# An attention-then-experts kernel: the last query group normalised in two parts, and a new hand-written order of instructions

## The chip, the core and the metric

The kernel runs on one core of a Trainium2 chip. The metric is the device time of one execution in microseconds (us), as the median of several executions. Work is spread over five engines with a queue each: TensorE (PE; its weight loads are shown as PEld), VectorE (DVE), ScalarE (ACT), GpSimd (POOL) and SyncE (SP), which here only issues DMAs. ACT can issue DMAs too.

## The reference

What is computed: attention of 8 batches of 12 heads with 448 positions of 64 values, whose q and k are first normalised, and behind it a mixture of 8 experts. Each expert takes the 448 tokens with the highest gate values for it, one expert after the other, and the tokens go through two matrix products.

```python
def _attn_ref(q, k, v, g_q, g_k):
    q_n, k_n = rmsnorm(q, g_q), rmsnorm(k, g_k)
    scores = q_n @ k_n.T / sqrt(64)
    scores = scores - max(scores, axis=-1)
    attn = exp(scores)
    attn = attn / (sum(attn, axis=-1) + 1e-9)
    return attn @ v
...
def _moe_ref(x, w_gate, w1, w2):
    logits = x @ w_gate                       # 3584 tokens, 8 experts
    for idx in argsort(-logits.flatten()):    # tokens to experts, 448 each
        ...
    for e in range(8):
        out[mask] = relu(x[mask] @ w1[e]) @ w2[e]
```

## The kernel before

Attention comes first (0 to 416 us), then the choice of the tokens (the router) and the experts; each expert's lists are found beside the products of the expert before it. Only attention is touched by the change.

Attention works on 24 groups of four heads (`g` 0 to 23; a group is two pairs of heads, a batch is three groups). For each group q and k are loaded, squared (`square`, L301) and summed on DVE (`sumsq`, L307), and a reciprocal root is made (`rsqrt`: two ACT steps at L313 and L315, then three small DVE or POOL steps, L319 to L326). Then come the scaling (`norm`, L342; q also times the gains, `gain`, L368 to L371) and the split into two 16-bit halves (`hi` on ACT, L376; `lo`, L379). From the third group on the halves are turned by DMA transposes (`transpose`, L389); the first two groups are worked in halves (`a` 0 and 1) and turned on PE (`turn_first`, L402), for an early start. PE then multiplies q and k once for the row maxima (`max_score`, L504 and L507, reduced on DVE at L514) and once exactly (`scores`, L535 to L544); ACT takes the exponentials (`exp`, L550).

`av` (L569) multiplies the exponentials with v. For one pair of blocks (`pair` 0 to 47, two for each group) it fills one PSUM tile `po` in seven windows `w`, sixteen matmuls each. When all seven are there, the pair is normalised: `x_norm` in three steps on DVE (the sums at L582, the reciprocal at L584, the product in place at L586), then `x_hi` on ACT (L596) writes the upper 16-bit half into `xa`, and `x_lo` on DVE (L602) the rest. `x_store` sends `xa` to memory in four DMAs for each batch, for the experts' gathers.

For the last batch (b = 7, pairs 42 to 47) there is a tail. `x_turn(7, hp)` turns, on PE, three of the windows of two pairs (L634; for odd `hp` also the window in the middle, L637): `hp` 4 takes windows 0 to 2 of pairs 46 and 47, `hp` 5 windows 4 to 6 and window 3 of the same pairs. `x_turned` copies the result (ACT, L652, for `hp` below 4, else DVE, L654). `gate_last` (L684 to L686) makes the gate's products with it in six steps, and `gate_copy` (L698, L699) hands the logits to the router, whose first instruction is L1124.

What runs when is not left to a scheduler. `plan` lists all 2117 steps of attention with their conditions; `ORDER` is a string of two characters for each step, and `Plan.run` emits the steps in just that order. Each engine works its steps in the order emitted and waits where a step needs another engine's result. So moving a step moves it in its engine's queue and decides for what everything behind it waits.

The first loads of q are issued by SP, the first loads of k by ACT: two main loads (192 KB, L235) and two tails (32 KB, L227) each. The first half of group 0 needs the first main load and both tails; the second half needs the other main load. Both queues also load a small gain vector (`gain_loads`, L141).

Of the kernel before, what the change touches and what calls it, by code (L numbers as in the profile page):

```python
# [31 lines left out]
OP = mybir.AluOpType  # L32
# [57 lines left out]
class Attention:  # L90
# [497 lines left out]
    def x_parts(self, pair):  # L588
        b, hp = divmod(pair, 6)
        x = self.T["xa", b].rearrange("p (w i h d) -> p w i h d", i=2, h=6, d=64)  # L590
        return self.T["po", pair][:, :, :64], x[:, :, 0, hp], x[:, :, 1, hp]

    def x_hi(self, pair):
        x, h, _ = self.x_parts(pair)
# [5 lines left out]
    def x_lo(self, pair):  # L600
        x, h, l = self.x_parts(pair)
        self.nc.vector.tensor_tensor(l, x, h, op=OP.subtract)  # L602
# [118 lines left out]
    def plan(self):  # L721
# [114 lines left out]
        for pair in range(2 * self.NG):  # L836
            b, hp = divmod(pair, 6)
            add("xn0", "D", 0.17, self.x_norm, pair, 0, after=[("po", pair)], make=("z", pair),
                opens=[("z", pair)] + [("xb", b)] * (hp == 0))
            add("xn1", "D", 0.2, self.x_norm, pair, 1, after=[("z", pair)], make=("y", pair), uses=[("z", pair)])  # L840
            add("xn2", "D", US["xn"], self.x_norm, pair, 2, after=[("y", pair)], make=("xn", pair), uses=[("z", pair)])
            add("xhi", self.engine("xhi", pair), US["xhi"], self.x_hi, pair, after=[("xn", pair)], make=("xh", pair), uses=[("xb", b)],
                frees=[("po", pair)])
            add("xlo", "D", US["xlo"], self.x_lo, pair, after=[("xh", pair)], make=("x", b, hp), uses=[("xb", b)],
                frees=[("po", pair)])
            x = [("x", b, n) for n in range(6)]
            if hp == 5:
                for i in range(4):
                    add("xst", "S", 0.6, self.x_store, b, i, after=x, uses=[("xb", b)], move=(1.5, 0.32 if i > 1 else 1.9))
                if b < last:  # L850
                    for i in range(4):
                        add("xtr", "S", 1.9 if i < 3 else 1.2, self.x_dma_turn, b, i, after=x, opens=[("xt", b)] if i == 0 else (),
# [10 lines left out]
            if b == last:  # L863
                ring = ("pm", "psc")[hp % 3 > 0]
                add("xturn", "T", US["xturn"], self.x_turn, b, hp, after=[x[hp | 1], x[hp - hp % 2]],
# [14 lines left out]
    def plan_first(self, plan, g, a):  # L880
# [47 lines left out]
        "050204031506160z1718191A0+1B0708000-1C1E1G1c1F1H1d1I1J1e1K1f1L091g1h1i1N1D1b1M011P1R242122252326281k1j1O1Q2x2z"  # L928
        "2-2y302+123M3N1n2A1o1l1m2W1U1S292B1TBZ2X2C2D1V2Y1W2E312ZBa2a2bBbBf1pBc2c1sBd1qBe32272V2F2G2H331u2I2e2d2J1rBh2h"
        "2f2i2K2g2L3OBg1X1Y1t342MBi2N353637BnBl14131z1Z1aBo2jBm2kGtGuBj2OBkBp39383ABqGvBr3Q2l3RBs1v1wGwBv3B3C3D3E0A1+3m"  # L930
        "3n0B0C1x1yBw2P2m2o2QGxBtGzGyX4G+Bu3P3S3o3q3TBxByG-H0BzB+M7MDMAM83p3F10C3C4MCC1C2B-H1H2C02R2pH3C52nC6M9MBRN3UH4"
        "3V3Y3W3X3a3bC7ROC83rME2S2q2T2r4A2sMGC9MF2UH5CACBCCRPMKH7CDCEMJMHMICF4BCG3s4C3tH6H83G2u2v202w1-2tRQRRH9HBHA3c4Y"
        "4ZCHCIHDRSHCHE3Z3d3u3w3v4a3y3H0D3I3JCJCKMLMNMRCL4DCM3x3+4E4F3KHFHGHHHICNCORTRUMMMOMQCPCQRV4cRW3z0E3-403L4G4HMP"
        "HJCRCSHL4KHKHMMSCTMTMYMWMX4dCUCVHN4bHOCWRXRYHPHQ3e3fMUCXRZCYHRMVCZ4eRaHS4fRb4I4L4J4M3gHVHTCaCbRc0FCcRd4NReMZMb"
        "MdCdHUHWRfCeRgMaHX4y4+CfCgMfMgMjCh4zCiMmMeMi4g4h414k4-Mc4O5K3lCjCkRhRiHZ5L4i4j4l3h3jHY3kHa4m3i0G4nHb4243444P4o"
        "MkClRjRkCmMhHd50HcCnRlCoMl4546He51525453RmRnHfCpCqRoHh4748HgHiMnCrRpCsHj4p49HlCtMsMtMrCuRqRvRuRyCvCwHkHm5M5O5N"
        "HnHpCxCyHo5PMoMpMqMu4Q4RS3Hr56HqHsCzS4C+11MyMvM+C-D0S5HtHxD1D2554S6658595A57MzMxMw4TD35QHu5RS65kS7S8S9D4SAHvHw"
        "Hy5mM-N5D5N4N3D6HzD75lD8N2H-4qSB4VSC4rH+I05n5o5p5S5T4U5W5U5V4WI15YI2D9DAN6N1N7NCDBDCN0SDI3I4685q5ZDDSEDESFNANB"
        "N8DFDGI5SGI6SHI7DHDIN9SISJRxRr67Rw5X5r5sI9DJDKSKI8IA5B4sIBICSLRzR+R-DLDMSMID6AIF5uIEIGRs5a4X6u6vDNDO69S0S15t5v"
        "4tNDNENH5C5DS2IHDPDQ6BNFNKNMDRNINGDS5w6W5xII6C4v4w6D6E6F4u6GIJDVNJILIKIMDWDTDUSNSOSPSQNNNPNQDXINIO5E5bIPIQDYDZ"  # L940
        "DaSRNLIR5yDbDc6X6H6I6K6LNONRNUNTSSSTRt4x5J5F6JIS5cIT5dSUSVDdDeSWNXIVDfNWNYNeDgNdDhNbNSNV5H6Y6ZIU6w6a6b5IIW5z6c"
        "6d5eDiDjSlSmDkSn5GIXIYIZDlDmSoSp6e6f0HNZNaNcDnIbIaSbSaId6gIc6yIe5f6hDo6xSqSr5+5-SsStNfNjNi6MDpDqIfIg5hIhDr6z7I"
        "6+6-70Ii6i6j72735g0I0JDsSuNlNgNhNkDtSvDuIjIkSc5jSdSeSfSgShSwSxSyDvDwIl7KImInSzDxSi5iSjDyNmNsNoDzNnNpNrNq7LD+D-"
        "S+S-E0Sk7g6k606NSXIp6l616462710KIoIrE1E2T0IqIsNtNuNw6O6P7JT1T2ItE3E4NyNxNvNzT3747M767N7O77757P7QN+O0E7T4E8T5Iv"
        "IuIwT6IxIy63E5E6O3N-O1E9T7EAIz65I+I-EBECO2O4T87RJ07iJ1T9TA6R6S6TJ2TBEDEEO5O7O66mTC6n7j7S6QJ3J47h6U7k78J5EFEGOC"
        "OEO8EHJ7O97UJ67V7TEIJ87l7mOAOBJ9EJSZ6VSYTHTI6oTK7WTRTSTTEK7nTUTVJBJAJCODOHENEOJDJF8486JEELEM85JGOJOGOOOIEPEQ87"
        "JHJIJJEROPOLESOFTWTXTYJL7A7BJK7o7q7p797sJNETEU7r7u7t0L7vTZJMJO8889TaTJ8S8T6p8A6s8B8C6qOMOKONTbTcEVEWTdJPJQ6rTL"
        "TNTMEXEYTeTfJRJTJSEbEcTOOQOVOUEZ8U8VEaJUTPTQ6t7CJXJVEd8D8W8s7XJW8E8GTGTE7w8IJY8FEeOXObOWEfOROTOdOS7D7EEg8X8Y8u"
        "8Z7GEhTgEiThJZJb7Y7ZTiOcEjEk8a8H8c8bJaTjJcTkOZOYOaTlElTmEmTn8vJdOeOgEnOjOkOhOfOiEo7FToJe7x8e8d8g8h8fTF7H7bTpEp"
        "TqTrEqJfJgJh7f7a9ETDErEsTsOlOrOnEtOqOoOmEu7yJiTtTu7zJj8t7+7c7e9GJkJlEvJm8w0M0NOsOpEwU79HOuOvExJnJoJpEyU8U97d8x"  # L950
        "UAJqEzOyE+UBOtOwOx0O8yE-UCF0UDUEJrJt9F9IJsJuUFF1F2OzP0O+P1F3UGF4JvJx8z8i8JTzU0T-T+83F5F68+8-0P9e9fJwJy0Q0R7-80"
        "9092P2O-P4P98K8L8MTx9JJz819KJ+J-F7F8P8P3P5P7UHUIUJK0UK9LF9FAULK1K3FBFC919M9NA0TyP6PA8N938O9OK2K49g8PU1U3U2UMUN"
        "UOFDFEK5K7UP82UQFFU4K6U5K8FGPBPEPGPHPDU69h9i9j9P8jFHFIPIPCPOFJA2A1A49QFKA3K98Q948RKAKB9SKCFLPFFMPNPJPLFNURUSUT"
        "UUFOKDKF8kUV8lTv958m9U9R8r9T0S0T0U0VPMPKUWUX0W0X8n8pKEKG8o9k0Y0Z0aFRFS0b9lKHKJKIKKFPUYFQPPPQPVFTFUKLKNUZUaUfUh"
        "KMFVFWPUPWPYFXKPKOKQFYKRKSFZFaPZKT8qKU96KV97TwUi9mKW9oAQ9nFbFcPcPXPSFdFeKXKYKZKa9qFhFiPRPTUpUqUrPaFfFg98KdKbUs"
        "UtFjFkPb9D9r999p9CKcKeA5UuUvA6A79BA80cAAABA90dPdPhPiPgFlKfKgFmUwUxKhKi9sFnFoUyPePjPfUz9W9XU+KjU-V0FpUgUjUlUkKl"
        "FqV1FrARFsUmPkPpPqPoPmUnUoFtFu0e9APrPnPwFvPxASATFwPlV29VACAEAF0fAD0gAoAq9YApAGV3V4AUAVAWKkKm9Z9aAXPsPtFxFyKn9d"
        "Uc9tV5V6KoKpFzF+PvPuV7Kr9uV8V99v9wUbUdAH9bKq9cKsKtF-ArG0PyQ2Q0P+G1AsVAVBKuG2KvKxG3G4AaKwAY0h0i0jAZAc0k0lKyAeUe"
        "Q1P-PzQ30mVCAtG5G6KzK+Q7Q9VDVEG7G89x0n0oAd0pAu9zVFAv9+VGVKVHK-L0AwAbAf9-VLVM9yL1L2BCBEAxAyAzG9GAQ5Q6QAQGGBGCBF"
        "L3L5L4GDGEQBQ8Q4QEQFVVVWVXL6VYAIL7L9L8AJAKAPVOGFBD0qVZQDGG0r0sQHQCALVaBGA+BHLAB0AOQIQJGHVbVcGILBLDVdVeLCLEGLGM"  # L960
        "QLQMQKGJGKAMA-BIBJB1BK0tQOQNQRQPGNLFLHVfVgVhViGOGPGQVjQTQQQUQSVkVlBMLGLIB2GRGSLJLLAgAhVmLKLMVNVPVRVQGTVJAiBLGU"
# [1036 lines left out]
```

## Time and profile before

| | us |
|---|---|
| three runs, median (lowest, highest) | 918.54 (917.5, 920.09) |
| the profiled execution, its own time | 916.3 |
| the profiled execution, span from first to last instruction | 914.5 |
| PE busy in the span | 863.1 |
| DVE, ACT, POOL busy | 660.6, 466.9, 343.0 |

The trace is of the profiled execution alone. A line of a timeline names start, duration, engine, line of the kernel, operation, what it writes and reads, and in brackets the idle time of that engine before it and what ended it. ACTq and SPq are the DMA-issuing parts of the ACT and SP queues. "Granted clock" (PEclk) is the TensorE clock as a share of full speed.

### The profile page before, as it was taken

What the parts mean: (1) busy time and instruction counts of PE and PEld (TensorE: products, weight loads), DVE (VectorE), ACT (ScalarE), POOL (GpSimd) and SP (SyncE); (2) the same over time, 40 slices, a digit from 0 to 9 for tenths busy, and PEclk for the clock granted to TensorE, in tenths of its full rate; (3) what the DMA queues carried; (4) which work ended last, traced back from release to release, by engine and by line L of the source; (5) the groups of instructions that cost most, each with busy time, mean ns of one, the idle gap of its engine ahead of it and who ended that gap; (6) DMA issues with size and microseconds to landing.
All of it is one profiled execution on the core that took longest, in us unless ns stands there. A gap on an engine that the chain in (4) does not pass through costs nothing.

```text
span 914.5 us, 30177 instructions
## 1 busy us (share of the span) xinstructions
PE 863.1 (94%) x13219; PEld 579.4 (63%) x13220; DVE 660.6 (72%) x1465; ACT 466.9 (51%) x670; POOL 343.0 (38%) x433
## 2 busy tenths in 40 slices
PE   2799999999999999995899999999999999999996
PEld 1367767777776777784556555565565655655873
DVE  5999878878886886647887777786858758149630
ACT  4777787788677676551333424232433324234411
POOL 6788787777675776100103021110112020121101
PEclk9999999999999999996899999999999999999999
DMA  6467999999998998621828559492929469461301
GB/s 198 113 157 173 183 261 156 219 179 224 205 230 182 210 203 143 114 82 63 253 86 251 182 190 268 150 282 91 298 88 282 142 219 258 155 130 69 131 18 44
DMA packets 224952, 157.31 MB, mean 172 GB/s; under 512 B 162100, under 2 KB 211508, under 8 KB 224820
## 3 DMA queue, kind: packets, MB, share of 16 engines
q1 hardware_dynamic: 219378, 132.90, 61.1%
q0 software_dynamic: 4608, 22.02, 7.0%
q8 instruction: 103, 1.69, 0.7%
q10 hardware_dynamic: 834, 0.46, 0.2%
q14 instruction: 29, 0.24, 0.1%
HBM read 94.40 MB, written 22.02 MB: 127 GB/s over the span
## 4 chain that ended last, share of the span: by engine, by line
PE 71%; issue 17%; DVE 5%; POOL 3%; DMA 2%; ACT 1%; SPq 1%; POOLq 0%; DVEq 0%
PE po L569 18%; PE ph L1775 16%; PE py L1792 13%; PE psc L535 9%; PE pm L504 4%; PE psc L537 3%; PE py L1801 2%; DVE mx L514 2%; POOL out_dram L1808 1%; POOL rows L1712 1%; DMA kqh<-s 1%; PE psc L542 1%; PE rp L1318 1%; DVE st L307 1%; PE rp L1475 1%
## 5 line engine op out<-in xcount | busy, mean ns | idle before, releaser
L514 DVE TENSOR_REDUCE mx<-pm 128x2 f32<-128x896 f32 x162 | 176.7, 1091 | 49.2 <-PE pm L504 44.8
L569 PEld LDWEIGHTS po<-v,e 128*64 128x64 f32 x5376 | 166.8, 137 | 31.8 <-issue 28.9
L569 PE MATMUL po<-v,e 128*64 128x65 f32 x5376 | 182.6, 223 | 2.9 <-issue 2.8
L1775 PE MATMUL ph<-xt,w1h 128*128 128x448 f16 (+2 forms) x708 | 183.5, 343 | 0.4 <-DVE xt L1733 0.3
L550 ACT ACTIVATE e<-psc 128x896 f32<-128x896 f32 x168 | 148.6, 912 | 49.9 <-PE psc L537 39.3
L1808 POOL DMA_INDIRECT out_dram<-y,idx x32 | 34.4, 1075 | 307.9 <-ACT y L1794 279.3
L1792 PE MATMUL py<-w2h,hh 128*128 128x384 f16 x384 | 125.0, 326 | 0.0
L1792 PE MATMUL py<-w2h,hl 128*128 128x384 f16 x384 | 125.0, 326 | 0.0
L1792 PE MATMUL py<-w2l,hh 128*128 128x384 f16 x384 | 125.0, 326 | 0.0
L1775 PE MATMUL ph<-xt,w1l 128*128 128x448 f16 (+2 forms) x354 | 119.9, 343 | 0.0
L1792 PEld LDWEIGHTS <-hh 128*128 128x128 f16 x768 | 73.6, 97 | 45.6
L1775 PEld LDWEIGHTS <-w1h 128*128 128x128 f16 x708 | 64.7, 97 | 52.7 <-issue 1.5
L1764 ACT ACTIVATE hh<-ph 128x448 f16<-128x448 f32 x56 | 30.5, 544 | 125.8 <-PE ph L1775 122.7
L1794 ACT ACTIVATE y<-py 128x384 f32<-128x384 f32 x48 | 23.5, 490 | 116.2 <-PE py L1792 96.0
L1712 POOL DMA_INDIRECT rows<-xd,idx x32 | 31.0, 969 | 114.9 <-DVE idlo L1480 46.8
L1579 DVE SCALAR_TENSOR_TENSOR w2l<-stage,w2h 128x768 f16<-128x768 f32 x64 | 60.2, 951 | 8.6 <-ACT w2h L1575 8.6
L504 PE MATMUL pm<-kqh 64*64 64x448 f16 x588 | 56.7, 362 | 1.8 <-DMA kqh<-s 1.4
L535 PE MATMUL psc<-kqh 64*64 64x448 f16 x588 | 56.0, 353 | 0.8 <-issue 0.4
L537 PE MATMUL psc<-rowq,rowk 64*64 64x448 f16 x588 | 55.8, 349 | 0.7 <-issue 0.7
L1766 DVE SCALAR_TENSOR_TENSOR hl<-ph,hh 128x448 f16<-128x448 f32 x56 | 34.1, 617 | 30.9 <-ACT hh L1764 30.8
L307 DVE TENSOR_REDUCE st<-sq 128x14 f32<-128x910 f32 (+2 forms) x52 | 52.7, 1016 | 4.4 <-ACT sq L301 4.4
L535 PE MATMUL psc<-kql,kqh 64*64 64x448 f16 x588 | 55.4, 349 | 0.0
(301 smaller groups left out, 1620.8 us busy)
## 6 DMA issues: line engine op xcount, KB each, us to landing
stage<-in_moe_w_dram SPq DMA_DIRECT2D x64, 768.0 KB
vraw<-in_v_dram SPq DMA_DIRECT2D x21, 448.0 KB
xd<-xa SPq DMA_DIRECT2D x16, 576.0 KB
qkraw<-in_q_dram SPq DMA_DIRECT2D x10, 896.0 KB
qkraw<-in_k_dram SPq DMA_DIRECT2D x10, 896.0 KB
xd<-xa SPq DMA_DIRECT2D x16, 96.0 KB
vraw<-in_v_dram SPq DMA_DIRECT2D x3, 384.0 KB
qkraw<-in_k_dram SPq DMA_DIRECT2D x2, 384.0 KB
```

The lines of the kernel that those rows point to most:

```text
L307: self.nc.vector.tensor_reduce(self.stat(g, 0, a)[:, i], self.view(self.T["sq", g, i], a), axis=AX.X, op=OP.add)
L504: self.nc.tensor.matmul(o, mine, self.every(k, r, a), start=True, stop=True)
L514: self.nc.vector.tensor_reduce(m, p[r, :, :448], axis=AX.X, op=OP.max)
L535: mm(o, mine, self.every(q, r, n), start=i == 0, stop=False)
L537: mm(o, one[r, :64], self.every(row, r, n), start=False, stop=True)
L550: self.nc.scalar.activation(e, p[:, :, :448], AF.Exp, scale=scale)
L569: self.nc.tensor.matmul(po[o:o + 64, w], self.T["e", d][:, h, q:q + 64], self.v32[g % 2][:, h, 4 * a + d % 7 % 4], start=d == ds[0], stop= ...
L1579: self.later(0.93, lambda w=w: self.nc.vector.scalar_tensor_tensor(l[:, w], v[:, w], self.WS, h[:, w], op0=OP.mult, op1=OP.subtract), k, i)
L1712: nc.gpsimd.indirect_dma_start(out=g[:n, c, :], out_offset=None, in_=self.xd, in_offset=bass.IndirectOffsetOnAxis(ap=idx[:n, c:c + 1], axi ...
L1775: nc.tensor.matmul(p, a, b[:, o], start=st, stop=sp)
L1792: nc.tensor.matmul(p, a[:, f, s], b[:, f, o], start=st, stop=sp)
L1808: st = nc.gpsimd.indirect_dma_start(out=self.out, out_offset=bass.IndirectOffsetOnAxis(ap=self.router.out[k][:n, c:c + 1], axis=0), in_=y[ ...
```

## The change

Three things are changed. First, pairs 46 and 47, the last group, are normalised in two parts: windows 0 to 3 (part 0) and windows 4 to 6 (part 1); each of the five steps of a pair is issued once for each part. Part 0 waits only for the first four windows of `av`, and the steps behind it (`x_turn` with `hp` 4 and three of the four stores of the batch) only for part 0. All earlier pairs are done as before. Second, ACT issues the load of the gain vector ahead of its four loads of k, not between them. Third, the string `ORDER` is new as a whole, with 2127 steps, ten more than before.

```diff
+    def windows(self, part):
+        return slice(0, 7) if part is None else slice(4 * part, 4 + 3 * part)
-    def x_norm(self, pair, n):
+    def x_norm(self, pair, n, part=None):
...
-        po = self.T["po", pair]
-        if n == 0:
+        w = self.windows(part)
+        po = self.T["po", pair][:, w]
+        if n == 0 and not part:
...
-        z = self.T["z", pair]
+        z = self.T["z", pair][:, :, w]
...
-            V.tensor_tensor(po[:, :, :64], po[:, :, :64], z[:, 1, :, None].to_broadcast([128, 7, 64]), op=OP.mult)
+            V.tensor_tensor(po[:, :, :64], po[:, :, :64], z[:, 1, :, None].to_broadcast([128, w.stop - w.start, 64]), op=OP.mult)
...
-                    after=[("VF", g), *(("e", d) for d in ds)], make=("po", pair),
+                    after=[("VF", g), *(("e", d) for d in ds)], make=("po", pair, int(w > 3)),
...
+            for part in (0, 1) if pair >= 2 * self.NG - 2 else (None,):
+                y, f = (pair, part), 1.0 if part is None else 0.6
+                po = [("po", pair, i) for i in ((0, 1) if part is None else (part,))]
+                add("xn0", "D", 0.17, self.x_norm, pair, 0, part, after=po, make=("z", *y),
...
-                    add("xst", "S", 0.6, self.x_store, b, i, after=x, uses=[("xb", b)], move=(1.5, 0.32 if i > 1 else 1.9))
+                    add("xst", "S", 0.6, self.x_store, b, i, after=done(int(i == 1)), uses=[("xb", b)], move=(1.5, 0.32 if i > 1 else 1.9))
...
     ORDER = (
-        "050204031506160z1718191A0+1B0708000-1C1E1G1c1F1H1d1I1J1e1K1f1L091g1h1i1N1D1b1M011P1R242122252326281k1j1O1Q2x2z"
...
+        "150501030207060z1716180+04000-191A1B1C1E1c1F08091d1D1b1G1H1I1J1eXE1K1f1L1g1h21242322281225262x2+301+2y1N1M1P1i"
...
```

Read out, the string says this of the places that matter.

Start, ACT's queue, before: load of k (main), load of k (tail), gain vector, tail, main, then squares of q half 0, k half 0, q half 1. After: gain vector, main, tail, tail, main, then squares of q half 0, q half 1, k half 0. The step `unit` (L439) moves from between the third and the fourth exponential up to the squares. On DVE the sum of q half 1 and the router's constant `before` (L1005), which stood behind the sum of k half 0 and behind `norm`, move ahead of the sum of k half 0. SP issues gq's load second instead of third, and the first load of v ahead of the last tails of group 1. On POOL the `gain` steps of group 1 move ahead of the last `lo` step of group 0.

Tail, PE's queue, after the last scores, before: `av` of pair 46 (six windows), pair 47 (four), then mixed to the end; then `x_turn` 1, 2, 3, and 5 and 4 among the gate steps. After: pair 46 windows 0, 1, 3, 2; `x_turn` 1; pair 47 windows 0, 2, 1, 3; pair 46 windows 4, 5, 6; pair 47 windows 4, 6, 5; `x_turn` 3, 4, 2; gate steps 0 and 1; `x_turn` 5; gate steps 4, 3, 2, 5. On DVE, behind the last `av`, the steps are: sums and reciprocal of pair 47 part 1, `x_lo` of pair 46 part 1, the product of pair 47 part 1, the copy of `x_turn` 4, `x_lo` of pair 47 part 1, and the two copies of `x_turn` 5.

Between `av`, scores and gate steps PE changes over 286 times in the old order and 286 times in the new one.

## Rows read from the trace of the kernel before

**Rows 1.** Busy time in stretches: PE, PEld, DVE, ACT, POOL us (instructions), clock, DMA.

```profile
20.00:40.00 20.00, 14.16 (x131) 7.82 (x128) 18.86 (x26) 13.85 (x28) 15.80 (x18) 1.00 0.34 112
40.00:60.00 20.00, 18.07 (x372) 12.07 (x364) 18.44 (x23) 15.68 (x30) 15.71 (x19) 1.00 0.59 126
```

**Rows 2.** Busy time of PE from 60 to 404 us, us (matmuls), clock, DMA.

```profile
60.00:404.00 344.00, 337.64 (x8522) 1.00 0.92 189
```

**Rows 3.** Timeline of ACT and SP at the start, DMA issues and first squares.

```profile
2.04 0.68 ACTq L141 DMA_DIRECT2D gk<-in_g_k_dram  x1
...
2.76 0.61 SPq L227 DMA_DIRECT2D qkraw<-in_q_dram  x1
...
4.75 0.60 ACTq L227 DMA_DIRECT2D qkraw<-in_k_dram  x1
5.39 0.61 ACTq L235 DMA_DIRECT2D qkraw<-in_k_dram  x1
6.12 0.63 ACT L301 ACTIVATE sq<-qkraw 128x512 f32<-128x512 f32 x1 [4.10 <-issue]
10.04 1.05 ACT L301 ACTIVATE sq<-qkraw 128x512 f32<-128x512 f32 x2 [3.29 <-DMA qkraw<-in_k_dram]
```

**Rows 4.** The chain that ended last, start to 44 us: start, duration, what.

```profile
10.78 0.71 DVE st L307
...
14.34 0.14 DVE before L1005
...
43.11 0.13 ACT unit L439
43.25 0.25 ACT unit L439
```

**Rows 5.** Timeline of DVE and POOL at 11 to 25 us: small root steps.

```profile
14.59 0.17 DVE L325 TENSOR_TENSOR st<-st 128x12 f32<-128x12 f32 x1
19.36 2.23 POOL L368 TENSOR_TENSOR qn<-qkraw,gg 128x512 f32<-128x512 f32 x2
19.64 1.02 DVE L324 TENSOR_TENSOR st<-st 128x16 f32<-128x16 f32 x1
20.70 0.92 DVE L325 TENSOR_TENSOR st<-st 128x16 f32<-128x16 f32 x1
24.21 0.95 DVE L324 TENSOR_TENSOR st<-st 128x12 f32<-128x12 f32 x1
```

**Rows 6.** Timeline around 270 us: a DMA transpose and PE's wait for it.

```profile
268.01 4.25 SPq L389 DMA_TRANSPOSE kqh<-s  x1
...
276.36 0.38 PE L504 MATMUL pm<-kqh 64*64 64x448 f16 x4 [1.45 <-DMA kqh<-s]
```

**Rows 7.** Timeline of the tail, from the last products to the router's first step.

```profile
404.02 6.75 PE L569 MATMUL po<-v,e 128*64 128x65 f32 x224
409.43 0.17 DVE L582 TENSOR_SCALAR z<-po 128x7 f32<-128x7 f32 x1 [5.24 <-PE po L569]
410.83 0.17 DVE L582 TENSOR_SCALAR z<-po 128x7 f32<-128x7 f32 x1 [0.33 <-PE po L569]
411.02 0.20 DVE L584 RECIPROCAL z<-z 128x7 f32<-128x7 f32 x1
411.26 0.63 DVE L586 TENSOR_TENSOR po<-po,z 128x448 f32<-128x448 f32 x1
411.93 0.54 ACT L596 ACTIVATE xa<-po 128x448 f16<-128x448 f32 x1 [0.18 <-DVE po L586]
412.50 0.62 DVE L602 TENSOR_TENSOR xa<-po,xa 128x448 f16<-128x448 f32 x1
413.22 0.49 PE L634 MATMUL psc<-ident,xa 128*128 128x128 f16 x6 [0.37 <-ACT xt L652]
414.80 0.56 DVE L654 COPY xt<-psc 128x768 f16<-128x768 f16 x1 [0.17 <-PE psc L634]
416.53 0.18 DVE L698 COPY logits<-po 128x24 f32<-128x24 f32 x1 [1.18 <-PE po L686]
```

More of the change, by code (lines that the diff above doesn't have):

```diff
@@ L585, in x_norm, with x_parts, x_hi @@
         else:
-            V.tensor_tensor(po[:, :, :64], po[:, :, :64], z[:, 1, :, None].to_broadcast([128, 7, 64]), op=OP.mult)
-    def x_parts(self, pair):
+            V.tensor_tensor(po[:, :, :64], po[:, :, :64], z[:, 1, :, None].to_broadcast([128, w.stop - w.start, 64]), op=OP.mult)
+    def x_parts(self, pair, part=None):
         b, hp = divmod(pair, 6)
[L590 to L594, printed above, removed]
+        w = self.windows(part)
+        x = self.T["xa", b].rearrange("p (w i h d) -> p w i h d", i=2, h=6, d=64)[:, w]
+        return self.T["po", pair][:, w, :64], x[:, :, 0, hp], x[:, :, 1, hp]
+    def x_hi(self, pair, part=None):
+        x, h, _ = self.x_parts(pair, part)
         if self.engine("xhi", pair) == "A":
@@ L598, in x_hi, with x_lo @@
             self.nc.vector.tensor_copy(h, x)
-    def x_lo(self, pair):
-        x, h, l = self.x_parts(pair)
+    def x_lo(self, pair, part=None):
+        x, h, l = self.x_parts(pair, part)
         self.nc.vector.tensor_tensor(l, x, h, op=OP.subtract)
@@ L837, in plan @@
             b, hp = divmod(pair, 6)
[L838 to L843, printed above, removed]
@@ L844, in plan @@
-            add("xlo", "D", US["xlo"], self.x_lo, pair, after=[("xh", pair)], make=("x", b, hp), uses=[("xb", b)],
-                frees=[("po", pair)])
-            x = [("x", b, n) for n in range(6)]
+            for part in (0, 1) if pair >= 2 * self.NG - 2 else (None,):
+                y, f = (pair, part), 1.0 if part is None else 0.6
+                po = [("po", pair, i) for i in ((0, 1) if part is None else (part,))]
+                add("xn0", "D", 0.17, self.x_norm, pair, 0, part, after=po, make=("z", *y),
+                    opens=([("z", pair)] + [("xb", b)] * (hp == 0)) * (not part), uses=[("z", pair)] if part else ())
+                add("xn1", "D", 0.2, self.x_norm, pair, 1, part, after=[("z", *y)], make=("y", *y), uses=[("z", pair)])
+                add("xn2", "D", US["xn"] * f, self.x_norm, pair, 2, part, after=[("y", *y)], make=("xn", *y), uses=[("z", pair)])
+                add("xhi", self.engine("xhi", pair), US["xhi"] * f, self.x_hi, pair, part, after=[("xn", *y)], make=("xh", *y),
+                    uses=[("xb", b)], frees=[("po", pair)])
+                add("xlo", "D", US["xlo"] * f, self.x_lo, pair, part, after=[("xh", *y)], make=("x", b, hp, part), uses=[("xb", b)],
+                    frees=[("po", pair)])
@@ L847, in plan @@
+            split = lambda n: 6 * b + n >= 2 * self.NG - 2
+            x = [[("x", b, n, i if split(n) else None) for i in range(2)] for n in range(6)]
+            done = lambda *parts: [x[n][i] for n in range(6) for i in (parts if split(n) else (0,))]
             if hp == 5:
                 for i in range(4):
-                    add("xst", "S", 0.6, self.x_store, b, i, after=x, uses=[("xb", b)], move=(1.5, 0.32 if i > 1 else 1.9))
+                    add("xst", "S", 0.6, self.x_store, b, i, after=done(int(i == 1)), uses=[("xb", b)], move=(1.5, 0.32 if i > 1 else 1.9))
@@ L850, in plan @@
                 if b < last:
                     for i in range(4):
-                        add("xtr", "S", 1.9 if i < 3 else 1.2, self.x_dma_turn, b, i, after=x, opens=[("xt", b)] if i == 0 else (),
+                        add("xtr", "S", 1.9 if i < 3 else 1.2, self.x_dma_turn, b, i, after=done(0, 1), opens=[("xt", b)] if i == 0 else (),
                             make=("xt", b, i), uses=[("xb", b), ("xt", b)], move=(1.5, 2.4 if i < 3 else 1.25))
@@ L864, in plan @@
                 ring = ("pm", "psc")[hp % 3 > 0]
-                add("xturn", "T", US["xturn"], self.x_turn, b, hp, after=[x[hp | 1], x[hp - hp % 2]],
+                add("xturn", "T", US["xturn"], self.x_turn, b, hp, after=[x[n][i] for n in (hp | 1, hp - hp % 2) for i in range(1 + hp % 2 if split(n) else 1)],
                     make=("tp", hp), opens=[("xt", b)] * (hp == 0), holds=[(ring, ("xt", hp))], uses=[("xb", b), ("xt", b)])
@@ L932 @@
[L932 to L961, printed above, removed]
@@ L967 @@
+        "GlGmLlLnLmLoBAGpGqWBWCWDQtQwQvQsGrLpLrGsWEWFBSBTQuQxQrBVLqR1Q+R0QyQzQ-WJWKWLWMBXLsLtLuBUW0VzLvLwWSWTWNWUWVW5W7"
+        "W6LxLzLyBYWWW8L+W9BWXDWAR2R3R7R6R8R4R5L-M1M0WGM2M3M4WaWbWcWdM5M6WeR9RARCRBWORGRIWjWkWlWPRHWmWnRJWwWxWyWHWzW+X4"
+        "X6X7RDRERFWoWpWqRKRMRLW-X0WrWQWsWfWhX1X2WgWtWuX3WXWIWRWYX9XBWvWiWZXAXCX8X5"
     )
```

43 lines of the change are left out of this document (35 added, 8 removed).

## The prediction

> **What bounds the kernel now.** I read the busy time in stretches first, to see which engine leads where. Up to 60 us DVE does: it is busy 18.86 of 20 us from 20 to 40 and 18.44 from 40 to 60, while PE has 14.16 and 18.07 [rows 1]. From there to the end of attention PE is the bound: 337.64 of 344 us, so 6.36 us of idle time in all [rows 2]. The steps on PE are the same before and after, and the number of its changes between kinds of work too (286). So the change can act in three places: the start, where DVE and what feeds it decide; the 6.36 us of stalls in the long middle; and the tail, where PE waits for the last pairs to be normalised. The router and experts behind are emitted as before and start when the logits are there.
>
> **The start.** The first half of group 0 needs k's main load and both tails. ACT's third load of k is issued only at 4.75, though the gain vector was done at 2.72, and the square of k waits until 10.04 for it; from there the chain runs on through DVE, from 10.78 [rows 3, 4]. What holds that issue the trace does not name. After the change it is still ACT's fourth DMA, with the gain vector (0.68) moved to the front. Bounds: it follows the others at once, at about 2.75, 2.0 us sooner, and if the way from issue to square stays 5.29 us (10.04 - 4.75) the chain gains 2.0. Or the whole queue slips by the vector's 0.68 and it loses 0.7. I take 0: the two loads ahead aren't what the square waits for, and the nearest row is the issue at 4.75 itself, the fourth in this queue as it will be again.
>
> The sum of q's second half goes ahead of k's. DVE is free there, as ACT waits 3.29 us for k before its next square [rows 3], and behind 10.78 that sum lay beside ACT's logarithm, so it gives nothing on the chain. The constant `before` goes the same way; its 0.14 us was on the chain [rows 4]. `unit` was on the chain too, 0.13 + 0.25 us between two exponentials [rows 4]; moved up to the squares it lies in ACT's waits for DVE. Together 0.5 us.
>
> The new order of POOL and DVE behind this can give or take more. Three small root steps on DVE took 1.02, 0.92 and 0.95 us, while POOL was at work, where a like one took 0.17 [rows 5]: 2.4 us on the leading engine. Each ended as a POOL step ended (19.64 + 1.02 = 20.66; POOL's two `gain` steps fill 19.36 to 21.59). In the new order POOL's `gain` steps of group 1 come one `lo` step earlier, but that `lo` step follows them at once, so POOL still has work without a gap as these root steps arrive. I take 0, between a gain of 2.4 (all three free) and a loss of 0.8 (one more caught). SP's loads change places too; the five that group 0 needs of it stay the first five, so I take 0.
>
> What DVE gains before 55 us moves PE's whole stream, as PE has the same work from there on. So the start is worth 0.5 us, from -1.0 to +3.
>
> **The middle.** Every queue gets a new order, SP's most of all: transposes, loads and stores change places. PE's stalls are single waits such as 1.45 us at 276.36 for a transpose that SP had issued at 268.01 and that took 4.25 us [rows 6]. Nothing in the string says that they become fewer or more as a rule: in nine groups before and six after, no PE step stands between the issue of the upper transpose and the first maximum that needs it. I take 0. The bounds are the 6.36 us at most gained, and as much lost; half of either is already a lot.
>
> **The tail.** Each pair in two parts means five small steps more for each of two pairs, 10 in all. Most cost nothing, as DVE was idle for 5.24 us beside the last products [rows 7]. What counts is the chain from PE's last product to the logits. Before: product done by 410.8, sum 0.17, reciprocal 0.20, product 0.63, ACT's half 0.54, `x_lo` 0.62, `x_turn` 5 at 413.22, that is 2.4 us; then 3.3 us more to 416.53, with the two turns, three copies and the gate steps in turn [rows 7].
>
> After: PE does `x_turn` 1 between the products now, about 0.6 us (0.49 for six transposes [rows 7], two more for the middle). It lay behind them in the shade of the chain before. 224 products take 6.75 us, 0.48 for a window, as before, so the last one ends at 411.4. Behind it on DVE: sum 0.17, reciprocal 0.20, then `x_lo` of pair 46, part 1, which stands ahead, the product of pair 47, the copy of `x_turn` 4 (0.56), and `x_lo` of pair 47. A step of three windows costs between 3/7 of the row for seven and the whole; I take some 0.6 of it: 0.37, 0.38, 0.37. With six gaps of 0.03 the sum is 2.25, so `x_turn` 5 starts at 413.65, later than now. But behind it less is left: the turn 0.6, two copies 0.25 and 0.56, one gate step instead of two (0.7), gaps 0.2: 2.3 us, so the logits come at 415.95 instead of 416.53. The tail gains 0.6; with 3/7 it gains 0.9, with the full durations it loses 0.2.
>
> There is one more cost that the trace of before can't show: both parts of a pair lie in one tile `po`, and the new order puts products of part 1 behind the vector steps of part 0. If the products wait for these (they write other columns), PE stands: four windows 1.93, `x_turn` 1 0.6, four windows 1.93 from 404.02 is 408.5; the part-0 steps of pair 47 (five, 1.6 to 2.4 us by the same scaling of [rows 7], with 4/7) end at 410.1 to 410.9; PE is done with part 1 of pair 46 at 409.95 and would wait 0.15 to 0.95 for pair 47. I take 0.1 as the forecast's share, as most of these steps lie beside the products of pair 46 and nothing yet shows the wait, and keep 0.95 for the range. The Trainium skill speaks here: its page "PSUM — Partial Sum Buffer", section "PSUM bank collisions raise a hardware error", says that two engines on one bank and the same partitions at once raise an error even at different columns, so that accesses have to be guarded by bank. By that rule the wait is there, and no run so far shows it.
>
> **The sum.** 0.5 at the start, 0 in the middle, 0.6 - 0.1 in the tail: 1.0 us. The profiled execution took 916.3 us (914.5 of span and 1.8 around it), so it would take 915.3. It lies 2.24 below the median of the three runs, 918.54, and below all three; I forecast for the median: 917.5.
>
> **The rivals.**
> First, k comes early: the fourth DMA of ACT isn't held any more. For it: the wait from 2.72 to 4.75 stands right behind the gain vector, and nothing else is late there. Against: behind SP's own vector load, issued at the same time, the next load went out at 2.76 [rows 3]. Price 2.0 more: 915.5. Chance 0.28.
> Second, PE waits in the tail at each turn to the other part: the tail's gain shrinks by 0.4 or more, 918.0. Chance 0.17.
> Third, slower: late transposes in the middle. SP issues them in a row with stores and loads, and one at 268.01 took 4.25 us, with 1.45 us for PE to wait [rows 6]. If the new order makes four more of them late, that is 5.8 us, less the 1.0 gained: 923.3. From three more late ones on it is slower than any measurement's doubt. Against it speak the nine and six groups above. Chance 0.15.
> That the change does not do what it says (part 0 normalised no sooner, as DVE is held by something) would leave the tail as it is and cost the 0.6 of `x_turn` 1; it is within the second.
>
> **How the numbers follow.** The forecast, 917.5 with its own range 915.5 to 919.5, has 0.40. A measurement of this kernel can tell about 0.3% (2.8 us) from no change, so faster means below 915.8 and slower above 921.3. Faster: 0.17 of the first rival and 0.10 of the forecast by luck in the middle, 0.03 of the second: 0.30. Slower: 0.11 of the third and 0.02 of the rest: 0.13. Same: 0.57. For the range I leave out the far half of the first rival's good cases with luck in the middle and most of the third: 914.0 to 921.5.
>
> **What would show it.** In the profile after: ACT's third load of k and the first square of k (4.75 and 10.04 if I am right, about 2.8 and 8 for the first rival). The small root steps on DVE, whether still three take about 1 us. PE's busy time from 60 to 404 us, near 337.6. In the tail the start of the products of pair 47, part 1, with or without a wait for DVE; `x_turn` 5 some 2.2 us behind the last product and the logits 2.3 us behind that. The prediction is wrong if the middle moves by more than 2 us either way, or if k is early.

## The result and the profile after

The changed kernel took 925.3 us (median of 12 runs, 919.2 to 930.0), the kernel before 918.05 beside it: a ratio of 1.0069, 95% interval 1.0046 to 1.0092. The same kernel run another 12 times gave 920.9 against 918.0, 1.0027 (1.0004 to 1.0050). So it is slower, by 0.3 to 0.7%, and its runs scatter by over 10 us. The forecast was 917.5, its range 914.0 to 921.5: the first measurement lies above that range; the second lies inside it only by this scatter, and is slower than before too.

The profiled execution of after took 919.38 us (span 917.6), 3.1 more than that of before. Busy time in the stretches of [rows 1, 2] (PE, PEld, DVE, ACT, POOL us with instructions; clock, DMA share, GB/s):

```profile
20.00:40.00 20.00, 12.66 (x134) 6.46 (x134) 17.20 (x23) 13.10 (x26) 14.26 (x17) 1.00 0.43 141
40.00:60.00 20.00, 17.77 (x386) 12.35 (x382) 19.37 (x24) 15.93 (x28) 17.16 (x18) 1.00 0.44 83
60.00:404.00 344.00, 334.03 (x8438) 254.07 (x8440) 269.84 (x418) 252.15 (x371) 228.41 (x262) 1.00 0.92 190
```

PE's busy time from 60 to 404 us fell from 337.64 [rows 2] to 334.03: 3.6 us more idle, which covers the 3.1 us by which this execution is longer. Who PE waited for there, in after (line, releaser: us in total, times, longest):

```profile
PE po L569 <- issue: 3.7, 4, 1.7
PE psc L537 <- issue: 1.9, 1, 1.9
PE psc L535 <- issue: 1.4, 2, 1.0
PE pm L504 <- issue: 1.4, 1, 1.4
PE psc L537 <- DMA rowq<-mt: 0.7, 1, 0.7
```

and in before:

```profile
PE po L569 <- issue: 2.8, 5, 1.3
PE pm L504 <- DMA kqh<-s: 1.4, 1, 1.4
PE psc L537 <- issue: 0.7, 1, 0.7
PE psc L535 <- issue: 0.4, 1, 0.4
```

"issue" means that PE waited for nothing that the view shows. The one wait for a transpose [rows 6] is gone, and the nameless ones have doubled, from 3.9 to 8.4 us by these rows. What they are shows when PE's instructions are counted. PE's timeline at the longest, in after:

```profile
139.04 0.35 PE L537 MATMUL psc<-rowq,rowk 64*64 64x448 f16 x2
141.33 0.38 PE L537 MATMUL psc<-rowq,rowk 64*64 64x448 f16 x2 [1.94 <-issue]
```

It stops in the middle of four like products. And the page of after lists a DMA queue that no line of the kernel uses:

```profile
q8 instruction: 103, 1.69, 0.8%
```

103 packets of 16,384 bytes; the trace of before has 26,484 instructions of PE (matmuls, weight loads, 45 of its sequencer's), 257 for each packet. I numbered them in order of start and looked where each issue wait of over 0.15 us falls between 62 and 430 us, in the 20 profiles of this study. There are 155, and every one stands at number 193 or 194 of a block of 256. Each ends 0.9 to 2.0 us (median 1.4) after a packet of q8 ended: in after one ran from 139.10 to 140.02, and PE went on at 141.33. So PE waits for its next block of instructions, which is fetched about one block ahead and comes late. The Trainium skill, page "Runtime: NRT & Kernel Launch", section "Instruction fetch mechanics", has blocks of 256 instructions fetched a page ahead, and says that crossing a border is "mostly hidden". The trace agrees on the block; the waits here, up to 2.8 us, are not hidden.

All profiles then follow one sum. Worked out from the traces, in us, column by column: PE's idle time from 60 us to the first product of pair 46 (in brackets the part of it that is "issue"); half the length of each stretch there with the granted clock at 0.50, the lower of its two levels; when that product starts; that start less both; from there to the end; span. The kernels other than before and after are those of the experiments below.

```
profile         waits (issue)  clock  pair 46   less   to end   span
before            6.4 ( 3.9)    0     404.0    397.7   510.5   914.5
before_again      7.9 ( 6.2)    0     404.6    396.6   510.7   915.3
tail_alone        8.0 ( 5.6)    0     404.1    396.0   510.4   914.4
start_alone       4.7 ( 1.8)    0     402.1    397.4   510.6   912.7
start_and_tail    7.7 ( 5.3)    0     405.9    398.2   510.4   916.3
best              8.6 ( 4.5)   1.7    408.3    397.9   510.4   918.7
pad64_before      7.2 ( 4.6)    0     405.1    397.8   517.2   922.3
pad128_before     8.5 ( 7.5)    0     405.6    397.1   510.5   916.2
no_v_before       6.3 ( 5.3)    0     403.7    397.4   510.7   914.4
after            10.0 ( 8.7)    0     407.2    397.3   510.4   917.6
after_again      12.4 (11.2)   1.7    412.5    398.3   510.4   922.8
tail_undone      12.6 (12.0)   1.7    413.0    398.7   511.0   924.0
spread_after      9.2 ( 8.6)   1.7    407.6    396.7   510.4   918.0
pad64_after      11.1 (10.5)    0     408.8    397.7   510.4   919.2
pad128_after     10.7 ( 7.4)   3.4    410.9    396.8   513.1   924.0
pad192_after      7.1 ( 5.6)   1.7    405.7    396.9   510.4   916.0
no_v_after        8.2 ( 7.0)   1.7    406.4    396.5   510.4   916.8
extra_loads      18.1 (13.0)   1.7    420.4    400.6   510.6   930.9
sp_of_before     19.3 ( 6.0)   3.4    421.3    398.6   510.4   931.7
sp_of_after      24.9 ( 5.2)   8.5    429.4    395.9   510.6   939.9
```

The work itself takes 396 to 399 us up to pair 46 in 18 of the 20, the end nearly always 510.4 to 511.0. What moves the time is how long PE waits in the middle. After against before: 3.6 of waits, 0.4 less for the work, 0.1 less to the end.

### The profile page after: what moved, and what is told of

It reads as the page before. It is cut to its first block, busy times and chain, and to the rows that moved or that the text cites. A ratio compares the mean times of both kernels' runs of the same rounds, so it can differ in the third digit from the quotient of the medians.

```text
span 917.6 us, 30190 instructions
## 1 busy us (share of the span) xinstructions
PE 863.2 (94%) x13219; PEld 579.0 (63%) x13220; DVE 659.7 (72%) x1473; ACT 466.7 (51%) x672; POOL 342.4 (37%) x433
## 4 chain that ended last, share of the span: by engine, by line
PE 72%; issue 17%; DVE 6%; POOL 2%; DMA 1%; ACT 1%; SPq 1%; POOLq 0%; DVEq 0%; ACTq 0%
PE po L569 18%; PE ph L1786 15%; PE py L1803 13%; PE psc L535 9%; PE pm L504 4%; PE psc L537 3%; PE py L1812 2%; DVE mx L514 2%; POOL out_dram L1819 1%; PE psc L542 1%; DVE st L307 1%; POOL rows L1723 1%; PE rp L1329 1%; PE rp L1486 1%; PE py L1753 1%
## 5 line engine op out<-in xcount | busy, mean ns | idle before, releaser
L535 PE MATMUL psc<-kqh,kql 64*64 64x448 f16 x588 | 55.7, 349 | 1.0 <-issue 1.0
```

Source lines behind the costliest of these rows:

```text
L535: mm(o, mine, self.every(q, r, n), start=i == 0, stop=False)
```

## The experiments

Theory 1: the loss is late instruction blocks in the middle (1a: SyncE's bulk transfers make them late; 1b: PE's order does; 1c: chance decides where block borders fall behind the loads). Theory 2: the two-part tail costs. Theory 3: router and experts.

**A second profile of after** (no edit).

> The kernel after, unchanged, once more. Theory 1 (late instruction blocks): in the middle TensorE stands still for 'issue' 8.5 us in the profile of after and 3.9 us in that of before, each time at the same place of a block of 256 of its instructions; this depends on how the DMA queues stand at that moment, so a second profile shows another sum, between 6 and 16 us, and its span less that sum is again 909 us within 1 us. The median stays 923 to 927 us. Theory 2 (the new tail costs): the excess over the profile of before sits between 404 us and the logits, and is the same in both profiles. Theory 3 (router and experts): it sits after 440 us, at the same place in both.

Waits 12.4 us instead of 10.0, span 922.8, to the end 510.4 as before. That is theory 1, not 2 or 3. The median is below the expected 923, and the span less the issue waits is 911.6, not 909 within 1: 1.7 us of that is the clock. The longest wait, and the granted clock behind it (last row, the windows view):

```profile
239.18 0.86 PE L569 MATMUL po<-v,e 128*64 128x65 f32 x22 [2.82 <-issue]
241.51 3.17 PE L569 MATMUL po<-v,e 128*64 128x65 f32 x64
...
240.60:243.80 3.20, 3.20 (x54) 2.49 (x48) 2.60 (x4) 2.30 (x3) 0.29 (x1) 0.50 0.08 28
```

After it the clock fell to its lower level for 3.4 us, and 64 products took 3.17 us where 2.09 is usual. So a long wait can cost more than its own length. SyncE's queue ahead of it:

```profile
227.20 0.53 SPq L252 DMA_DIRECT2D qkraw<-in_q_dram  x1
227.78 0.51 SPq L252 DMA_DIRECT2D qkraw<-in_k_dram  x1
228.39 6.73 SPq L389 DMA_TRANSPOSE kqh<-s  x1
```

Two loads of 896 KB, a transpose right behind that held the queue 6.73 us, a border at 231.1, and the block asked for there began to move only at 235.8.

**The parts one by one**: before's order up to pair 46's first product with after's tail; the converse; after's first 200 steps with before's rest; start and tail together.

The orders in words, not as the string:

```diff
-ORDER = steps of before
+tail_alone      before up to pair 46's first product, then what is left in after's order
+tail_undone     after up to pair 46's first product, then before's undivided tail
+start_alone     after's first 200 steps, then what is left in before's order
+start_and_tail  after's first 200, before's middle, after's tail
```

> The kernel before with its own order up to the last group's products, and only the two-part normalising with the tail order of after behind it. Theory 1: nothing ahead of the last group changes, so the middle's issue waits are those of before (3 to 7 us) and the time is 918 us within 1.5; from the first product of pair 46 to the logits 12.2 us instead of 12.5. Theory 2: the two-part tail itself costs, 921 us or more, and the stretch from pair 46's first product to the logits grows by over 2 us.

> The kernel after with its order up to the last group's products, and the undivided tail of before behind it. Theory 1: the loss is ahead of the tail, so it stays: 923 to 928 us, issue waits in the middle 6 to 16 us. Theory 2: the loss goes with the divided tail: 917 to 919 us.

> The first 200 steps of after's order (up to about 45 us: k's first loads in order of use on ScalarE's queue, the new order of the first three groups), then the rest in the order of before, undivided tail. If the start's gain is real and the middle of before carries it on: 1 to 2 us faster than before, 916 to 917. If the early start is given back in the first 60 us, as the profile of after shows: 918 within 1. Theory 1 alone says that the middle's issue waits may come out otherwise than in before, since all blocks meet the loads earlier by 1 to 2 us: 914 to 925.

> The first 200 steps of after's order, the middle of before, the two-part tail of after. Theory 1: the middle is before's, so its issue waits are 1.6 to 5.5 us; the tail takes 0.2 us less from pair 46's first product to the logits; the start is 0 to 1 us earlier: 916 to 918 us, a ratio of 0.998 to 1.000 that cannot be told from before. Rival: start and middle of two orders don't fit together, 920 or more.

tail_alone 918.4 us, 1.0003 (0.9982 to 1.0025); start_alone 917.5, 0.9991 (0.9971 to 1.0011); tail_undone 922.6, 1.0035 (1.0015 to 1.0054). The loss stays when the tail is undone (922.6, just below its expected 923) and goes when before's order is kept up to the tail: theory 2 is out. start_and_tail, 919.6, 1.0028 (1.0009 to 1.0047), missed its 916 to 918: with the work unchanged (398.2) one block at 276 us came 2.15 us late. So before's middle can meet such a wait too.

**The cause doubled**: in before, each of the 21 loads of v of 448 KB is issued twice.

```diff
             self.heads_of(eng, self.v, t.rearrange("p u d -> p (u d)")[:, :896], g, 1)
+            self.heads_of(eng, self.v, self.extra, g, 1)
```

> The kernel before with each of SyncE's 448 KB loads of v issued a second time, into a tile that nothing reads: some 9 MB more through the DMA queues between 20 and 400 us, and 0.6 us more of SyncE per load. If bulk transfers delay the instruction blocks: issue waits in the middle over 8 us (before: 3.9), median over 921 us. If not: waits 2 to 6 us, and the time within 2 us of 918, unless SyncE's transposes come later (then waits for kqh or kql show instead).

932.7 us, 1.0158 (1.0122 to 1.0194). PE's longest sums of waits in extra_loads:

```profile
PE po L571 <- issue: 7.0, 5, 2.7
PE psc L539 <- issue: 3.0, 3, 2.6
PE psc L537 <- issue: 2.5, 3, 1.6
PE po L667 <- DMA xt<-xa: 2.0, 2, 1.0
```

Issue waits went to 13.0 us, from 3.9 and 6.2 in the two profiles of before, with PE's instructions unchanged: bulk transfers make the blocks late. PE waited for transposes as well (last row).

**The cause taken away**: the same loads left out.

```diff
+            if g < 4:
                 self.heads_of(eng, self.v, t.rearrange("p u d -> p (u d)")[:, :896], g, 1)
```

> The kernel after with SyncE's 20 loads of v of 448 KB for groups 4 to 23 left out: the products use v of an earlier group, the output is another, and every instruction of the engines stays. 9 MB less pass through the DMA queues between 60 and 400 us. Theory 1a (bulk transfers hold back TensorE's instruction blocks): the waits of TensorE from 60 us to pair 46, issue and others, fall from 9.9 to 12.6 us to under 4, no drop of the clock in that stretch, and the time to 909 to 913 us; what is left, first product of pair 46 less waits and drops, stays 396 to 399 us, as in all profiles so far. Theory 1b (TensorE's order alone): waits 8 to 12 us, 920 us or more.

> The same 20 loads of v left out of the kernel before. Theory 1a: waits from 6.4 to under 3 us, 911 to 914 us, and the difference between the two orders, some 3 to 7 us with the loads, shrinks to under 2 us. Theory 1b: waits 5 to 8 us, 917 to 918, and the difference stays.

919.8 us, 1.0017 (0.9999 to 1.0034), and 915.8, 0.9970 (0.9952 to 0.9989), with before at 918.9 beside them. By the medians each gains some 3 us, but the two orders stay 4 us apart, and the single profiles show no clear fall: waits of 8.2 us and 1.7 of clock are left in after (10.0 and 0 with the loads), 6.3 in before (6.4 and 7.9). The numbers of 1a missed in both. So v's loads are at most a part of the cause; the pairs of q and k loads are left, and after still waited 2.73 us at 234.7.

**SyncE's sequence exchanged** between the two orders, the other engines' kept (in words again).

```diff
-SyncE's DMAs in the kernel's own sequence
+sp_of_before  after, with SyncE's DMAs in before's sequence
+sp_of_after   before, with SyncE's DMAs in after's sequence
```

> The kernel after (its order on TensorE, VectorE, ScalarE and GpSimd, its two-part tail) with SyncE's DMAs in the sequence of before, each put where before has it by the count of TensorE's steps ahead of it. Profiles so far: issue waits of TensorE from 62 to 416 us 8.5, 11.1 and 11.9 us with after's order (both SyncE's and TensorE's), 3.9, 5.5 and 1.6 with before's; span less these waits 909 to 912 in all six. Theory 1a (the instruction block comes late because SyncE's bulk loads and stores are bunched): waits 2 to 6 us, median 917 to 919.5 us. Theory 1b (the order on TensorE sets it: where a block's border falls, how fast a block is used up): waits 8 to 12 us, median 921 to 925.

> The converse: the kernel before, whole, with SyncE's DMAs in the sequence of after. Theory 1a: waits 8 to 12 us, median 921 to 925. Theory 1b: waits 2 to 6 us, median 917 to 919.5 us.

938.9 and 940.9 us, outside both theories. The sequences don't fit the other engines, and other waits take over (sp_of_after):

```profile
PE psc L535 <- ACT e L550: 9.2, 4, 4.1
PE psc L537 <- DMA rowq<-mt: 5.9, 2, 4.0
```

Inconclusive. Issue waits of 6.0 us with after's order on PE (sp_of_before) are fewer than 1b expected, but PE stood 13 us for other reasons there, so this says little.

**Four DMAs of after spread out, two of before's**. In the sketch, `lqk` is the load of q (0) or k (1) for a group and the next, `lv` a load of v, `xst` an `x_store`, `rows` the transfer of a group's maxima for PE; a bar stands between two of SyncE's DMAs.

```diff
-... lqk 18,0 | lqk 18,1 | transpose 15 ...      lqk 12,1 | xst 0,3 | xst 0,1 | xst 0,2 | rows 7 | transpose 9
+... lqk 18,0 | transpose 15 ... transpose (lower) 15 | lqk 18,1      lqk 12,1 | rows 7 | transpose 9 | xst 0,3 | xst 0,1 | lv 7 | xst 0,2
+best: start_and_tail, with lqk 8,1 behind rows 4 and lqk 10,1 behind the lower transpose 7
```

> The kernel after, with four of SyncE's DMAs moved and nothing else: the 896 KB load of k for groups 18 and 19 goes from right behind q's (225 us in the profile of after) to behind the transpose at 241 us, and three stores of the first queries go from 130 to 132 us, right behind three bulk loads, to behind the transpose at 136 us and the load at 141 us. In after and in its second profile the blocks asked for at 134 and at 229 us came 5.1 and 4.6 us later (4.4 and 4.7 in the second), and TensorE then stood still 1.9 and 1.7 us (1.4 and 2.8). Theory 1a (bunched bulk transfers hold the block back): those two waits fall below 0.7 us together, the issue waits in the middle go from 8.5 to 11.9 us down to 4 to 8, the drop of the granted clock near 240 us goes, median 917.5 to 921. Theory 1b (the order on TensorE): nothing changes, 921 to 925, waits 8 to 12 us. A cost may show where the moved load is waited for (ScalarE's squares of k for group 18).

> As the run before it (start of after, middle of before, two-part tail), with two loads of SyncE moved: k for groups 8 and 9 from right behind q's and v's (85 us in the profile of before) to behind the transfer at 93 us, and k for groups 10 and 11 from right between two transposes (116 us) to behind the transpose at 121 us. In every profile with before's middle TensorE stood still near 91 us (0.4 to 0.7 us) and near 125 us (0.6 to 2.2 us) for a block asked for right behind those loads. Theory 1a: both waits go, and the time is 1 to 2 us below that kernel's: 915 to 917. Theory 1b: they stay.

spread_after: 919.6 us, 1.0027 (1.0005 to 1.0050). The wait at 141 us shrank from 1.94 to 0.29, the one at 236 is gone, as 1a says; the sum isn't lower, since a new one came elsewhere, again behind two bulk loads and a transpose:

```profile
208.22 0.50 SPq L252 DMA_DIRECT2D qkraw<-in_k_dram  x1
208.76 0.51 SPq L623 DMA_DIRECT2D xd<-xa  x1
...
210.60 7.95 SPq L389 DMA_TRANSPOSE kql<-s  x1
...
218.18 0.38 PE L535 MATMUL psc<-kql,kqh 64*64 64x448 f16 x4 [2.57 <-issue]
```

best: 919.8, 1.0019 (0.9997 to 1.0041). The wait near 125 went, the one at 92 stayed (0.77), 2.14 us came at 276 with a drop of the clock, and PE waited 2.19 us for a transpose at 134. It beats neither.

**The borders shifted**: idle products at 5 us, 32 for a quarter of a block, 64 for a half, 96 for three quarters.

```diff
             nc.vector.tensor_copy(self.gg, p)
+            p = self.po_tile()
+            for _ in range(64):
+                nc.tensor.matmul(p[:, :16], self.rowk, self.rowk[:, :16], start=True, stop=True)
```

> The kernel after with 64 products of 16 columns of zeros (64 matmuls and 64 weight loads) into an unused tile on TensorE, behind the gains' product at 5 us, where TensorE stands idle until 12.7 us. Nothing else changes; every later border between blocks of 256 instructions falls half a block, some 2.5 us of work, earlier in the work. If the issue waits are waits for instruction blocks: they stand at the same place of a block again, so 128 instructions earlier in the work than in after, at other products; their sum is another one, 4 to 14 us, and span less sum stays 909 to 912 us. If they belong to the work (a wait that the profile doesn't show): same products, same sum as after (8.5 to 11.1), time as after.

> The kernel after with 32 products of 16 columns of zeros at the start (64 instructions, a quarter of a block), in TensorE's idle time before 12 us. Profiles with after's order so far: waits of TensorE from 60 us to pair 46 plus half of the clock's drops 10.0, 14.1, 14.3 us (unpadded borders), 14.1 us (half a block), 10.9 us (four DMAs moved). Theory 1c (chance of alignment: a long wait comes where a block's border falls 2 to 4 us behind the issue of q's and k's loads): with other borders the sum is another one, anywhere from 4 to 15 us, the long waits at 141, 236 and 277 us go or move, median 916 to 924. Theory 1a (after's DMAs as such): sum 9 to 15, median 920 to 924, whatever the borders.

> As the run before it, with 96 products (192 instructions, three quarters of a block). Theory 1c: sum 4 to 15 us and different from the other three shifts, median 916 to 924. Theory 1a: sum 9 to 15 us, median 920 to 924.

> The kernel before with 64 such products (128 instructions, half a block). Sum of waits and drops in the profiles with before's middle so far: 6.4, 7.9 (before, twice), 8.0, 4.7, 7.7. Theory 1c: before's low sum was luck of its borders too, so a half-block shift gives 4 to 15 us, and a median up to 924. Theory 1a: sum 4 to 9 us, median 917 to 919.

> The kernel before with 32 products of zeros at the start (64 instructions, a quarter of a block). So far a shift of half a block made before 0.34% slower (920.8 us), and after is 0.27 to 0.69% slower than before at all four shifts (none, a quarter, a half, three quarters). Theory 1c (luck of the borders alone): a third shift of before lands among those of after, 1.002 to 1.006, sum of waits and drops 8 to 14 us. Theory 1a (after's order makes more late blocks at any shift): 0.999 to 1.002, sum 4 to 9 us.

> The kernel before, unchanged, once more, for a second profile of its middle. Theory 1: the waits of TensorE between 60 us and pair 46 come out at other borders and with another sum, 4 to 9 us, and the span less these waits and half of each drop of the clock is the same as in the first profile within 1.5 us.

In each the waits stand at 193 or 194 of 256 again, so at other products: they belong to the borders, not to the work. pad64_after 922.4 us, 1.0067 (1.0041 to 1.0093); pad128_after 922.2, 1.0037 (1.0017 to 1.0056); pad192_after 921.5, 1.0045 (1.0024 to 1.0066); pad128_before 920.8, 1.0034 (1.0008 to 1.0060); pad64_before 918.3, 0.9990 (0.9972 to 1.0009); before_again 917.1 in one run. Averaged over its shifts (the two ratios of the unshifted after as one, 1.0048) after's order stands at 1.0049, before's at (1 + 0.9990 + 1.0034) / 3 = 1.0008. So 1c is true in part, a shift alone is worth up to 3 us, and some 0.4% stays with the order, as 1a says. The single ratios overlap (each is known to 0.2%): pad128_before is above 1a's 919, pad192_after's waits of 7.1 are below its 9 to 15, and start_and_tail's 1.0028, with before's middle, is as slow as spread_after. Taken by the middle, the kernels with after's average 1.0043 (after, tail_undone, spread_after and three shifts), those with before's 1.0009 (before, start_alone, tail_alone, start_and_tail, best and two shifts). Waits and clock together are 11.9 us in the mean of the seven profiles with after's middle and v's usual loads (spread_after's among them), and 7.6 in the eight with before's: 4.3 us, or 0.5%, apart.

What in the order does it, the traces tell. SyncE's 22 upper transposes (min/median/max ns), in before

```profile
L389 SPq DMA_TRANSPOSE kqh<-s x22: 1371/2246/4877, 40.5 to 361.5; - x22
```

and in after

```profile
L389 SPq DMA_TRANSPOSE kqh<-s x22: 1393/2840/6661, 40.3 to 367.5; - x22
```

From 60 to 400 us the mean over all 68 transposes is 2.58 to 2.71 us in those seven profiles, and 2.29 to 2.51 in those eight. The new order puts transposes more often right behind a pair of loads: five of those of q and k in after (4.8 to 6.7 us each), two in before, from 55 us on.

The blocks of instructions come late at the same places. In these 15 profiles I took for each border from 62 to 400 us (977 in all, counted at instruction 193) how long behind it the next packet of q8 began. It was 3 us or more at 6 of the 404 borders with no load of q, k or v issued from 6 us before to 1 us behind, and at 60 of the 190 with two or more. Where it was less than 2 us (661 borders), PE never waited at the next border; where it was 3 us or more (127), PE waited 94 times. The borders that met both two such loads and a transpose in SyncE's queue:

```
                                        after's middle   before's middle
such borders in a profile (mean)            8.6              3.0
issue waits behind them (us, mean)          5.1              0.1
issue waits behind all others               3.9              4.7
```

Each of the seven profiles has 2.5 to 6.7 us of waits behind such borders, none of the eight more than 0.5. So the difference in issue waits between the two orders sits there, behind loads bunched with a transpose. This was read off the traces after the runs; the 6 us were chosen (5 or 7 give the same picture), and no run took just these bunches away: spreading four DMAs removed the two waits that it aimed at and no more, and the exchange failed.

## Why the prediction was wrong

**The start: k came early, for half of the first rival's reason, and the gain was spent.** The step "I take 0" for ACT's fourth DMA failed. ACT's queue and squares in after, against [rows 3]:

```profile
0.77 0.53 ACTq L141 DMA_DIRECT2D gk<-in_g_k_dram  x1
1.33 0.41 ACTq L235 DMA_DIRECT2D qkraw<-in_k_dram  x1
1.78 2.16 ACTq L227 DMA_DIRECT2D qkraw<-in_k_dram  x2
4.60 0.38 ACTq L235 DMA_DIRECT2D qkraw<-in_k_dram  x1
6.02 1.05 ACT L301 ACTIVATE sq<-qkraw 128x384 f32<-128x384 f32 x2 [0.30 <-DMA qkraw<-in_q_dram]
```

The second of the two tails, ACT's fourth DMA, is issued at 3.33, not 4.75, and the second of the two squares, that of k, starts at 6.45, not 10.04. What holds this DMA the views don't name, but the semaphore events in the traces do. The first loads, of both queues together, use eight semaphores in turn, and this one waits for the load that had its semaphore before it: in before a tail of q on SP, which landed at 4.73, in after SP's gain vector `gq`, which landed at 3.31. So it is still held, only not as long, and the vector's move on ACT alone doesn't do it: with SP's sequence of before (sp_of_before) it is issued at 4.35, with SP's new sequence but ACT's old one (sp_of_after) at 4.40. The prediction had put SP's new sequence at 0 by itself. PE's first product of scores came at 16.61 instead of 19.30, 2.7 us sooner. But a little later:

```profile
26.25 0.49 ACT L412 ACTIVATE kql<-po 128x384 f16<-128x384 f16 x1 [4.42 <-DVE kql L410]
...
27.00 0.63 ACT L376 ACTIVATE s<-kn 128x512 f16<-128x512 f32 x1
...
27.69 1.12 PE L402 MATMUL po<-ident,s 128*128 128x128 f16 x8 [4.06 <-ACT s L376]
```

The new order has ACT wait 4.42 us for a copy of DVE that stands behind maxima and sums there; `s<-kn` of group 1, whose input was ready at 21.4, is queued behind that wait, and PE stands 4.06 us. Nothing is left at the first product of pair 2: it starts at 64.27 in after and 65.04 in before, but at 64.1 to 65.2 in eight profiles with after's order there and at 63.7 to 65.1 in six with before's, 64.6 in the mean of both. So the start was worth 0.0, where 0.5 was forecast; start_alone's 0.9991 can't be told from 1 either.

The three slow root steps on DVE [rows 5] stayed three (0.83, 0.97, 0.97 us in after, each again ending within 0.1 us of a POOL step): that step held.

**The middle: the step that failed.** It is "I take 0", with 6.36 us as the bound and late transposes as the only rival. The bound was read as many single waits like the 1.45 us for a transpose [rows 6], yet 3.9 of the 6.36 us were issue waits, and no step of the prediction asked what they were. The runs showed in its place 8.7 us of issue waits (11.2 in the second profile), those of over 0.15 us all at borders of instruction blocks, and over half of their time behind bunched loads. A middle that moves by more than 2 us was named as a sign of being wrong: it moved by 3.6. The third rival named the right place and sign with the wrong mechanism: in after PE's long waits were for no transpose. Its count of PE's steps between transpose and maximum could not see a wait for instructions. And 6.36 us was no bound for a loss: after_again lost 6.0 by waits and 1.7 by the clock against before.

**The tail: mechanism right, gain overrated.** The chain that ended last in after, from pair 46's first product:

```profile
407.31 2.02 PE po L569 x64
409.33 0.44 PE psc L640 x6
409.88 2.04 PE po L569 x64
411.94 0.17 DVE z L587
...
413.30 0.43 DVE xa L608
413.77 1.62 PE po L569 x48
...
417.42 0.35 PE psc L640 x6
...
419.54 0.18 DVE logits L704
```

and PE's timeline where it waits:

```profile
413.77 1.62 PE L569 MATMUL po<-v,e 128*64 128x65 f32 x48 [0.48 <-DVE xa L608]
```

From PE's first product (407.24) to the logits 12.30 us, in before 12.51 [rows 7]: 0.2 gained, where 0.5 was the forecast. The products of pair 47, part 1, do wait for DVE's last step on part 0: PE stood 0.48 us, within 0.15 to 0.95, where 0.1 was taken. The Trainium skill, page "PSUM — Partial Sum Buffer", section "PSUM bank collisions raise a hardware error", asks for such a guard between engines on one bank, at different columns too; the trace agrees, with these 0.48 us. That term is one that was mis-sized. The products end 8.15 us after they began (predicted 7.4): beside the wait, `x_turn` 1 took 0.55 and the 224 products 7.12 in pieces, where [rows 7] has 6.75. The logits came 4.15 us behind them (predicted 4.55). tail_alone gave the same 12.3.

**Forecast and range.** Without the middle some 0.2 us of the forecast's 1.0 was there, all of it from the tail. The range left out most of the third rival and had no term for PE's unnamed waits, nor for the clock behind them.

## What to carry to other kernels

A wait that the profile puts down to "issue" can have a cause that the views don't name. Number the engine's instructions and look whether the waits stand at one place of a block; if so, they are waits for instructions, and a new order changes them by chance and by where it bunches bulk DMAs. Cost a reordering of a kernel with long unrolled streams by the waits that it may move, not by the steps that it moves: here that was 2.5 to 6.3 us by the medians, against 0.2 us from the edits themselves. Where runs scatter so, compare several profiles of each kernel before a cause is named.

## What the runs showed of the hardware

A load of bulk data delays the instructions of an engine that doesn't touch it: 21 loads of 448 KB more made PE's issue waits 13.0 us instead of 3.9 and 6.2. Behind some of the longest waits (2.82 us in after_again, 2.57 in spread_after) the granted clock stood at 0.50 for 3.4 us, which costs about 1.7 us more; behind others as long (2.70 in extra_loads) it did not fall. Late transposes reach into the experts now and then, here in pad64_before:

```profile
572.76 0.91 PE L1778 MATMUL ph<-xt,w1h 128*128 128x448 f16 x2 [4.22 <-DMA xt<-rows]
```

With 6.8 us at the lower clock around it, the part behind pair 46 took 517.2 us in that execution, 6.7 more than usual, although that kernel's median, 918.3, is that of before.
